# Issue order of two weight groups, one step on VectorE and the count of filler products in the opening of a fused mLSTM and gated MLP kernel

## The chip, the cores and the metric

The kernel runs on one core of a Trainium2 chip. The metric is the time of one execution on the device in microseconds (us). The median of three runs of the kernel before is 516.91 us (516.87 to 516.94).

## The reference

An mLSTM cell (4 batches, 8 heads, 768 steps, head dimension 40) is followed by a gated projection. With x the cell's output as 3072 rows of 320:

```python
for t in range(S):
    m_new = np.maximum(f_gate[:, :, t] + m, i_gate[:, :, t])
    f_stab = np.exp(f_gate[:, :, t] + m - m_new)
    i_stab = np.exp(i_gate[:, :, t] - m_new)
    C = f_stab * C + i_stab * outer(v[t], k[t])
    n = f_stab * n + i_stab * k[t]
    y[t] = sigmoid(o_gate[t]) * (C @ q[t]) / max(abs(n . q[t]), 1)
h = x @ w_in                 # 320 x 2048
out = (h * np.cos(h)) @ w_out  # 2048 x 320
```

All is float32.

## The kernel before, in words

The 768 steps are cut into six chunks of 128. A *cell* n is one chunk of one batch: n = 4 * chunk + batch, 24 cells in all. A cell needs a matrix of decay weights E (loaded as rows of running maxima from DRAM, then exponentials on ScalarE), the scores (`scores`, PE, tile `ps`), their product with E (`weigh`, VectorE), the values (`values`, PE, tile `vt`), the state's increment (`seam`, PE, tile `pu`; `state`, VectorE adds it or ScalarE copies it) and the gated, normalised result xT (`turn_gates`, VectorE).

The projection works on a whole chunk, 512 columns, in eight steps `Up(c, 0)` to `Up(c, 7)`, two tiles `pup` each. For each tile ScalarE rounds (`near`), VectorE takes the rest (`rest`), ScalarE takes the sine (`sin`), and VectorE multiplies (`gate`, tile `g`). `down(c, k)` multiplies g with two 128-row blocks of w_out on PE (16 products of 320 columns, tile `po`, in chunk 0). While a chunk's projection runs, the next chunk's cells are computed between its steps.

The opening loads the weights as well, and works on their bits before they are used: w_in in four groups (`weights_in(0)` to `weights_in(3)`, eight DMAs of 128 KB and two of 128 KB for the low rows each), w_out in eight pieces (`weights_out(0)` to `weights_out(7)`, one DMA of 640 KB each). A piece passes through `take_apart` (two passes on ScalarE, L154 and L156), `bound` (two on VectorE, L160 and L161) and `put_together` (one on VectorE, L167, one on GpSimd, L168); `convert_out()` does all three for the oldest piece of w_out still waiting. Piece p of w_out is used first by `down(0, p)`, group 3 of w_in by `Up(0, 6)`. w_out's pieces rotate through three buffers (the first of them used once for other data before), so piece p waits for piece p - 3; w_in's groups rotate through two.

The program is written under a manual schedule: each engine runs its instructions in the order in which the code issues them, and waits on semaphores where data or a buffer is needed. All loads of this part are issued by SyncE, in order, on one hardware queue.

`warm(k)` issues k products of a tile of zeros (bf16, 128 x 512, L1016, tile `pw`), whose result nobody reads. `gates_turn()` transposes gate tables on PE (L289, L290, tiles `pg`, `pd`), and `gates_keep` copies them on ScalarE. `normalize(3)` is VectorE's work on cell 3 (L621 to L629, tile `y`), `seam(3)` its transposes and increments on PE (L663, L665, L673). `first_cells` is followed by `first_chunk`, in which the projection of chunk 0 runs beside cells 4 to 7.

Of the kernel before, what the change touches and what calls it, by code (L numbers as in the profile page):

```python
# [29 lines left out]
def kernel(  # L30
# [667 lines left out]
    def state(n, part=slice(0, 4), on_dve=False):  # L698
        if n < N - B:
            for j, r, s, w in list(halves(n))[part]:  # L700
                u = increment(n, r, w)
                s = like(s, u)
                if n < B:
                    (nc.vector.tensor_copy if on_dve else nc.scalar.copy)(out=s, in_=u)
                else:
                    nc.vector.tensor_tensor(out=s, in0=s, in1=u, op=OP.add)
# [306 lines left out]
    def warm(k, bank=None):  # L1013

        for _ in range(k):
            nc.tensor.matmul(bank or pw, nil, nil.unsqueeze(1).to_broadcast([128, HP, 128]), start=True, stop=True)  # L1016

    def first_cells():
        gates_in()
        nc.scalar.copy(out=ident_b, in_=ident)  # L1020
        load(0, "qk")
        later_gates_in()
        load(0, "v")
        load(1, "qk")
        load_o(0, (0, 1))
        load(1, "v")
        load(2, "qk")
        load_E(0)
        load_E(1)
        warm(12)  # L1030
        wall_in(0, 0, pmu)
        wall_in(0, 1, psum_o())
        gates_first()
        fill()
        clear_low()
        gates_first_out()
        spread(0, 0)
        decay_exponents_half(0, 0)
        turn(0)
        turn_out(0, False)  # L1040
        gates_sums()
        spread(0, 1)
        decay_exponents_half(0, 1)
        decay(0)
        weigh_k(0)
        load_E(2)
        load(2, "v")
        load_E(3)
        load_o(0, (2, 3))
        load(3)  # L1050
        pieces.extend(weights_in(0))
        wall_in(1, 0, psum_o())
        wall_in(1, 1, psum_o())
        gates_less_sums()
        spread(1, 0)
        decay_exponents_half(1, 0)
        scores(0)
        gates_maxima()
        turn(1)
        weigh(0)  # L1060
        sigmoid(0, slice(0, 2))
        turn_out(1, False)
        spread(1, 1)
        decay_exponents_half(1, 1)
        gates_exponents()
        decay(1)
        weigh_k(1)
        values(0)
        normalize(0)
        scores(1)  # L1070
        turn(2)
        turn_out(2, False)
        gates_exp()
        warm(2)
        seam(0)
        weigh(1)
        seam_out(0)
        state(0)
        load_E(B, and_G=False)
        load_one(B)  # L1080
        decay_exponents(2)
        gates_diagonal()
        decay(2)
        weigh_k(2)
        values(1)
        load_G(B)
        normalize(1)
        scores(2)
        turn(3)
        sigmoid(0, slice(2, 4))  # L1090
        seam(1)
        load(B, "kv")
        outs.append(weights_out(0))
        weigh(2)
        decay_exponents(3)
        turn_out(3)
        seam_out(1)
        values(2)
        decay(3)
        weigh_k(3)  # L1100
        state(1)
        normalize(2)
        warm(2)
        scores(3)
        warm(1)
        seam(2)
        weigh(3)
        take_apart(*pieces[0])
        bound(pieces[0][0])
        put_together(*pieces.pop(0))  # L1110
        values(3)
        decay_exponents(B)
        pieces.extend(weights_in(1))
        seam_out(2)
        state(2)
        for piece in pieces[0:2]:
            take_apart(*piece)
        warm(3)
        pg = gates_turn()
        normalize(3)  # L1120
        gates_keep(*pg)
        bound(pieces[0][0])
        put_together(*pieces.pop(0))
        warm(2)
        seam(3)
        seam_out(3)
        outs.append(weights_out(1))
        load_o(1)
        load_E(B + 1, and_G=False)
        load_one(B + 1)  # L1130
        load(B + 1, "kv")
        load_G(B + 1)
        outs.append(weights_out(2))
        low_dimensions_of(B)
        turn_blocks(B)
        bound(pieces[0][0])
        put_together(*pieces.pop(0))
        state(3, on_dve=True)
        decay(B)
        scale_q(B)  # L1140
        odd_values_of(B)
        weigh_k(B)
        ahead.append(weights_in(2))
# [12 lines left out]
    def convert_out():  # L1156
        piece = outs.pop(0)
        take_apart(*piece)
        convert(*piece)
# [16 lines left out]
    def first_chunk():  # L1176
        n = B
        up = Up(0, 0, lambda: scores(n))
        weigh(n)
        sin_next()  # L1180
        nears(up)
        rests(up)
        sines(up)
        values(n)
        seam(n)
        convert_out()
        outs.append(weights_out(3))
        load_two(n + 2)
        load_E(n + 2)

        up = Up(0, 1)
        full = pieces[0:2]
        low = pieces[2]
        for piece in (*full, low):
            take_apart(*piece)
        for piece in (*full, low):
            bound(piece[0])
        put_together(*full[0])
        nears(up)
        rests(up)  # L1200
        put_together(*full[1])
        sines(up)
        put_together(*low)
        state(n)
        ahead.append(weights_in(3))
        down(0, 0)

        up = Up(0, 2)
        convert_out()
        outs.append(weights_out(4))  # L1210
        load_E(n + 3)
        low_dimensions_of(n + 1)
        turn_blocks(n + 1)
        sigmoid(1)
        nears(up)
        decay_exponents(n + 1)
        rests(up)
        scale_q(n + 1)
        weigh_k(n + 1)
        odd_values_of(n + 1)  # L1220
        sin_next()
        sines(up)
        denominators(n)
        gate_over(n)
        down(0, 1)

        for x in range(2):
            m, f2 = n + x, 3 + 2 * x
            *full, low = ahead.pop(0)
            convert_out()  # L1230
            outs.append(weights_out(5 + 2 * x))
            if x == 1:
                load_two(n + 4, "Kv")
                load_E(n + 4)
            turn_gates(m)
            up = Up(0, f2)
            scores(m + 1)
            take_apart(*full[0])
            decay(m + 1)
            convert(*full[0])  # L1240
            nears(up)
            take_apart(*full[1])
            rests(up)
            convert(*full[1])
            fade(m)
            low_out(m)
            sin_next()
            weigh(m + 1)
            sines(up)
            take_apart(*low)  # L1250
            convert(*low)
            down(0, f2 - 1)
            values(m + 1)
            seam(m + 1)
            if x == 1:
                load_E(n + 5)

            up = Up(0, f2 + 1)
            convert_out()
            if x == 0:  # L1260
                outs.append(weights_out(6))
                load_two(n + 4, "qk")
            else:
                load_o(2)
            state(m + 1)
            if x == 0:
                low_dimensions(n + 2)
                odd_values(n + 2)
            turn_blocks(m + 2)
            decay_exponents(m + 2)  # L1270
            weigh_k(m + 2)
            scale_q(m + 2)
            nears(up)
            rests(up)
            denominators(m + 1)
            sines(up)
            down(0, f2)
            gate_over(m + 1)

        n = 2 * B - 1  # L1280
        convert_out()
        turn_gates(n - 1)
        convert_out()
        up = Up(0, LAST)
        scores(n)
        decay(n)
        fade(n - 1)
        low_out(n - 1)
        decay_exponents(n + 1)
        weigh_k(n + 1)  # L1290
        odd_values(n + 1)
        nears(up)
        rests(up)
        sin_next()
        weigh(n)
        sines(up)
        turn_blocks(n + 1)
        decay(n + 1)
        down(0, LAST - 1)
        values(n)  # L1300
        seam(n)
        load_two(n + 3, "qk")
        load_E(n + 3)
        load_two(n + 3, "Kv")
        for _ in range(6):
            next(last_down)
        denominators(n)
        gate_over(n)
        sigmoid(2)
        sin_next()  # L1310
        turn_gates(n)
        scale_q(n + 1)
        state(n)
        fade(n)
        weight_sums(0)
# [142 lines left out]
```

## Time and profile before

| | |
|---|---|
| median of three runs | 516.91 us (516.87 to 516.94) |
| the profiled execution | 514.89 us |
| its span, first to last instruction | 512.9 us |
| TensorE (PE) busy | 500.8 us (98%) |
| VectorE (DVE) busy | 405.7 us (79%) |
| ScalarE (ACT) busy | 286.3 us (56%) |
| GpSimd (POOL) busy | 247.1 us (48%) |
| mean granted TensorE clock | 0.992 |
| DMA moved | 57.99 MB, of it most in the first 130 us |

The profile is of one execution. A busy engine is one that has an instruction of the program in it; PEld is TensorE's weight load, SPq the issuing of DMAs by SyncE. Idle time of an engine that isn't the bottleneck costs nothing; what matters is who waits last, and the chain of waits follows that back from the end. PEclk is the share of the full clock that TensorE was granted. In lists of waits the columns are the time in total, the number of waits and the longest one.

### The profile page before, as it was taken

What the parts mean: (1) busy time and instruction counts of PE and PEld (TensorE: products, weight loads), DVE (VectorE), ACT (ScalarE), POOL (GpSimd) and SP (SyncE); (2) the same over time, 40 slices, a digit from 0 to 9 for tenths busy, and PEclk for the clock granted to TensorE, in tenths of its full rate; (3) what the DMA queues carried; (4) which work ended last, traced back from release to release, by engine and by line L of the source; (5) the groups of instructions that cost most, each with busy time, mean ns of one, the idle gap of its engine ahead of it and who ended that gap; (6) DMA issues with size and microseconds to landing.
All of it is one profiled execution on the core that took longest, in us unless ns stands there. A gap on an engine that the chain in (4) does not pass through costs nothing.

```text
span 512.9 us, 14114 instructions
## 1 busy us (share of the span) xinstructions
PE 500.8 (98%) x5564; PEld 358.2 (70%) x5564; DVE 405.7 (79%) x831; ACT 286.3 (56%) x550; POOL 247.1 (48%) x413
## 2 busy tenths in 40 slices
PE   9999999899999999999999999999999999999995
PEld 5865554546567787777677777677697677677775
DVE  6898897898598888888878888878878778654644
ACT  3888893957945548635537736538736531323230
POOL 9743645455686585454455354454343333121212
PEclk9989999899999999999999999999999999999999
DMA  9999999998612823922723743733652000001001
GB/s 139 236 204 229 248 188 271 247 207 195 107 55 58 180 79 84 176 58 58 198 45 102 170 74 98 190 56 98 158 86 100 2 6 6 1 1 52 1 2 53
DMA packets 97650, 57.99 MB, mean 113 GB/s; under 512 B 62336, under 2 KB 89056, under 8 KB 97584
## 3 DMA queue, kind: packets, MB, share of 16 engines
q1 hardware_dynamic: 95888, 55.31, 48.8%
q0 software_dynamic: 1360, 1.43, 1.1%
q8 instruction: 44, 0.72, 0.6%
q10 hardware_dynamic: 336, 0.34, 0.2%
q14 instruction: 22, 0.18, 0.1%
HBM read 51.71 MB, written 4.11 MB: 109 GB/s over the span
## 4 chain that ended last, share of the span: by engine, by line
PE 85%; DVE 9%; DMA 2%; issue 1%; ACT 1%; POOL 0%; SPq 0%; DVEq 0%
PE pup L724 32%; PE acc L724 24%; PE pup L783 4%; PE late L724 4%; PE po L822 4%; PE ps L530 4%; PE vt L565 2%; PE vt L556 2%; PE ph L546 2%; PE pw L1016 1%; PE pup L777 1%; PE pu L673 1%; DMA bits<-in_moe_w_in_dram 1%; DVE g L806 1%; DMA bits<-in_moe_w_out_dram 1%
## 5 line engine op out<-in xcount | busy, mean ns | idle before, releaser
L794 ACT ACTIVATE n<-pup 128x512 int32<-128x512 f32 x96 | 52.2, 593 | 179.0 <-PE pup L724 166.5
L724 PE MATMUL pup<-xT,w_in_sb 64*128 64x512 f32 x608 | 147.9, 595 | 0.2 <-DVE g L806 0.2
L797 DVE SCALAR_TENSOR_TENSOR n<-pup,n 128x512 f32<-128x512 f32 x96 | 61.9, 686 | 70.5 <-ACT n L794 70.2
L877 POOL TENSOR_TENSOR D<-g 128x128 f32<-128x128 f32 x40 | 18.9, 473 | 135.1 <-DVE g L806 125.8
L724 PEld LDWEIGHTS pup<-xT,w_in_sb 64*128 64x128 f32 x608 | 59.1, 187 | 35.6 <-issue 32.8
L802 ACT ACTIVATE n<-n 128x512 f32<-128x512 f32 x96 | 58.6, 629 | 14.3 <-DVE n L797 14.3
L806 DVE SCALAR_TENSOR_TENSOR g<-pup,n 128x512 f32<-128x512 f32 x96 | 62.1, 681 | 2.5 <-ACT n L802 1.2
L724 PE MATMUL acc<-w_out_sb,g 64*128 64x160 f32 x624 | 63.6, 296 | 0.0
L724 PE MATMUL acc<-T,g 64*128 64x160 f32 x624 | 61.7, 296 | 0.0
L724 PEld LDWEIGHTS acc<-w_out_sb,g 64*128 64x128 f32 x624 | 55.4, 187 | 8.6 <-issue 8.5
L724 PEld LDWEIGHTS acc<-T,g 64*128 64x128 f32 x624 | 54.0, 187 | 9.7 <-issue 8.9
L453 ACT ACTIVATE E<-E,tab 128x128 f32<-128x128 f32 x160 | 49.0, 388 | 1.3 <-POOL E L439 1.1
L679 POOL DMA_DIRECT2D xL<-xT x38 | 21.3, 562 | 51.6 <-DVE xT L609 40.6
L724 PE MATMUL pup<-xL,w_in_l 64*128 64x512 f32 x152 | 40.2, 589 | 0.0
L724 PE MATMUL acc<-T,S 64*128 64x160 f32 x312 | 39.5, 296 | 0.0
L724 PE MATMUL acc<-w_out_sb,S 64*128 64x160 f32 x312 | 39.2, 296 | 0.0
L822 PE MATMUL po<-w_out_sb,g 128*128 128x320 f32 x128 | 38.4, 454 | 0.4 <-POOL w_out_sb L168 0.4
L783 PE MATMUL pup<-xT,w_in_sb 128*128 128x512 f32 x80 | 37.3, 607 | 0.3 <-DVE xT L609 0.3
L530 PEld LDWEIGHTS ps<-t,t 40*128 40x128 f32 (+1 forms) x384 | 25.5, 187 | 13.8 <-issue 4.9
L822 PEld LDWEIGHTS po<-w_out_sb,g 128*128 128x128 f32 x128 | 24.6, 197 | 13.2 <-issue 1.7
L724 PEld LDWEIGHTS acc<-w_out_sb,S 64*128 64x128 f32 x312 | 30.4, 187 | 3.1 <-issue 3.1
L724 PEld LDWEIGHTS late<-w_out_sb,D 64*128 64x128 f32 x320 | 28.7, 187 | 4.9 <-issue 4.2
(204 smaller groups left out, 959.7 us busy)
## 6 DMA issues: line engine op xcount, KB each, us to landing
E<-M_d SPq DMA_DIRECT2D x22, 512.0 KB, 3.7
qr<-in_q_dram SPq DMA_DIRECT2D x34, 160.0 KB, 3.4
kr<-in_k_dram SPq DMA_DIRECT2D x34, 160.0 KB, 4.4
bits<-in_moe_w_out_dram SPq DMA_DIRECT2D x8, 640.0 KB, 6.6
G<-G_d SPq DMA_DIRECT2D x18, 256.0 KB, 5.5
bits<-in_moe_w_in_dram SPq DMA_DIRECT2D x32, 128.0 KB, 5.0
out_dram<-o_sb SPq DMA_DIRECT2D x22, 160.0 KB, 4.0
o<-in_o_gate_dram SPq DMA_DIRECT2D x40, 80.0 KB, 4.1
```

The costliest lines, as they stand in the source:

```text
L453: nc.scalar.activation(out=Es[n][:, h], in_=Es[n][:, h], func=AF.Exp, scale=-1.0, bias=tab[:, c, 0, g:g + 1])
L530: nc.tensor.matmul(ps[j][:, p], kT[r, p], qT[r, p], start=True, stop=True)
L546: nc.tensor.matmul(ph[:, h], E[:, h], vs(n)[:, h, 0:D1], start=True, stop=True)
L679: nc.gpsimd.dma_start(out=xL[c][64 * e:64 * e + 64, b], in_=ys[n][0:128:2])
L724: ins = nc.tensor.matmul(a, lhs[r], rhs[r], start=start, stop=stop).ins
L783: nc.tensor.matmul(pu.rearrange("p (b t) -> p b t", b=B), w_in_sb[:, i, ts(part_of(f2, e), 128)], xT[c][:, i:NK * B:NK], start=(i == 0 and ...
L794: nc.scalar.activation(out=self.n[e], in_=self.pu[e], func=AF.Copy, bias=0.25)
L797: nc.vector.scalar_tensor_tensor(out=self.n[e].bitcast(FP), in0=self.pu[e], scalar=0.25, in1=self.n[e], op0=OP.add, op1=OP.subtract)
L802: nc.scalar.activation(out=r, in_=r, func=AF.Sin, scale=TWO_PI_DOWN)
L806: nc.vector.scalar_tensor_tensor(out=g, in0=self.pu[e], scalar=TWO_PI, in1=self.n[e].bitcast(FP), op0=OP.mult, op1=OP.mult)
L822: nc.tensor.matmul(po[c][b], gs[c, f][:, ts(b, C)], w_out_sb[:, f], start=(f == 0), stop=(f == NF - 1))
L877: tt(out=D1, in0=G0[:, 1, 1], in1=G1[:, 1, 1], op=OP.add)
```

## The change

Three edits in the opening.

- `first_cells`: `warm(3)` ahead of `gates_turn()` becomes `warm(6)`, and `warm(2)` ahead of `seam(3)` becomes `warm(1)`: three products of zeros more ahead of the gate transposes, one less behind them.
- `first_chunk`: `state(4)` (n is 4 there) moves from ahead of `down(0, 0)` to behind the `convert_out()` of w_out's second piece. On VectorE its four additions come behind the three bit operations of the piece instead of ahead of them.
- `first_chunk`: the ten DMAs of w_in's last group move behind the one of w_out's fifth piece in SyncE's order.

```diff
@@ first_cells
         for piece in pieces[0:2]:
             take_apart(*piece)
-        warm(3)
+        warm(6)
         pg = gates_turn()
         normalize(3)
         gates_keep(*pg)
         bound(pieces[0][0])
         put_together(*pieces.pop(0))
-        warm(2)
+        warm(1)
         seam(3)
         seam_out(3)
@@ first_chunk
         put_together(*full[1])
         sines(up)
         put_together(*low)
-        state(n)
-        ahead.append(weights_in(3))
         down(0, 0)
 
         up = Up(0, 2)
         convert_out()
+        state(n)
         outs.append(weights_out(4))
+        ahead.append(weights_in(3))
         load_E(n + 3)
         low_dimensions_of(n + 1)
         turn_blocks(n + 1)
```

ScalarE's and GpSimd's orders are the same in both programs.

## The prediction

> **What bounds the kernel now.** I read the page first, then PE's waits, then the chain of waits around the longest of them, then stretches of the clock, then the engines' timelines.
>
> ```profile
> span 512.9 us, 14114 instructions
> PE 500.8 (98%) x5564; PEld 358.2 (70%) x5564; DVE 405.7 (79%) x831; ACT 286.3 (56%) x550; POOL 247.1 (48%) x413
> PEclk9989999899999999999999999999999999999999
> ```
>
> TensorE is busy all the time, so an edit is worth what it takes from PE's idle time, or from the time in which PE runs at a lower clock: slices 3 and 8 of 40 show an 8. Who lets PE wait:
>
> ```profile
> PE ps L530 <- DVE xT L609: 2.4, 1, 2.4
> ...
> PE po L822 <- POOL w_out_sb L168: 0.4, 1, 0.4
> ```
>
> One wait of 2.4 us is nearly all that can be had. The chain (start, us, what) shows where it comes from:
>
> ```profile
> 77.10 6.21 DMA bits<-in_moe_w_in_dram
> ...
> 83.37 5.83 DMA bits<-in_moe_w_out_dram
> ...
> 89.23 0.79 ACT w_out_sb L154
> ...
> 92.74 0.57 DVE xT L609
> 93.31 0.04 issue
> 93.36 1.16 PE ps L530 x16
> 94.52 6.19 PE po L822 x16
> ```
>
> w_out's fifth piece is issued at 83.37, behind the ten DMAs of w_in's last group, and lands at 89.20. ScalarE, done with the gates at 84.30, waits 4.9 us for it; VectorE waits for ScalarE, its product xT comes at 93.3, and PE, done with the projection at 90.99, waits for that. Then the clock (stretch, us, PE busy, PEld, DVE, ACT, POOL, clock, DMA share, GB/s):
>
> ```profile
> 30.47:33.87 3.40, 3.40 (x34) 2.86 (x31) 3.18 (x9) 3.34 (x11) 1.24 (x1) 1.00 1.04 196
> 33.88:37.28 3.40, 3.40 (x43) 1.93 (x43) 3.04 (x6) 2.25 (x8) 1.64 (x3) 0.50 0.89 135
> ...
> 91.91:95.30 3.39, 1.95 (x19) 1.65 (x20) 3.08 (x6) 3.38 (x9) 1.63 (x2) 1.00 1.17 210
> 95.32:98.72 3.40, 3.40 (x8) 2.12 (x7) 2.54 (x5) 3.38 (x6) 1.19 (x1) 0.50 1.21 210
> ```
>
> Two stretches of 3.41 us run at half clock; I cut the windows at their edges. They start 61.44 us apart, 18 times their length. The one at 95.3 follows a stretch in which PE had 1.95 us of work. The one at 33.9 follows one without a gap, but filled by small products (16 with 41 columns, ten 32x32 transposes) and only three of 512 columns.
>
> **The change, part by part. 1. The fifth piece ahead of w_in's last group.** The built order shows the one w_out DMA before the ten w_in DMAs, nothing else moved on SyncE.
>
> ```profile
> 76.07 5.49 SPq L177 DMA_DIRECT2D bits<-in_moe_w_in_dram  x8
> ...
> 83.37 0.39 SPq L188 DMA_DIRECT2D bits<-in_moe_w_out_dram  x1
> ```
>
> So its issue moves from 83.37 to about 76.1. Its buffer was the second piece's, which GpSimd left at 60.0: no new wait. Ahead of it remain the rows of E and G, landed by 81.25 (the issue eight behind). Each issue goes on with the landing of the eighth before it: 83.37 comes right after w_in's third DMA landed at 83.31 (77.10 + 6.21). The piece's 640 KB take 2.3 us at the 280 GB/s that this stretch moves (80 to 90 us), 3.4 us at the 194 of the ten us before; it lands at 83.6 to 84.7, about when ScalarE wants it (84.3).
>
> VectorE is free at 86.65 and starts the piece's bit work then, 3.4 us before its 90.05; xT comes at 89.9, ahead of PE's 90.99. **The 2.36 us go.** What is late next: w_in's first half. Its fourth DMA landed by 83.85 (the eighth issue after it); put back by 2.3 to 3.4 us, 86.2 to 87.2. From ScalarE's first pass over it (90.59) to VectorE's last weighing of E (100.11) were 9.5 us, so E would be ready at 95.7 to 96.7, its first half 0.6 us earlier. PE would have done scores (1.1) and the fifth down step (4.5) by 96.6 and wants the first half then. No wait, 0.5 us at the worse end once the other terms have pulled PE forward. I take none, since 280 is the rate of the stretch itself. The second half and the low rows (wanted at 92.5 and about 96) land by 89.2, when the piece landed before, because the sum of bytes is the same. All later transfers keep their place; the sixth to eighth piece landed by 92.6, 95.9 (issues eight behind) and 104.2 and are wanted at 96, 105 and 106 on the shifted clock: over 1 us of slack each.
>
> **2. The clock behind that wait.** Without the gap, the stretch before 95.3 holds 3.4 us of work instead of 1.95. The down step took 6.19 us at half clock; its like at 107.41 took 4.50. **1.69 us go**, if the clock follows PE's work.
>
> The Trainium skill ("TensorE: Matmul & The Clock Gate", the table of its section on why this matters for your kernels) says that half clock comes after idle gaps of over some 3 us. The trace differs: 2.36 us were enough at 91, and no gap at all at 33.9. The same page (Part 1) has a free-running window of 3413 ns, with which the two stretches agree.
>
> **3. Cell 4's state behind the second piece's bit work.**
>
> ```profile
> 55.54 0.85 DVE L706 TENSOR_TENSOR st<-st,pu 40x128 f32<-40x128 f32 x4
> ...
> 57.48 0.83 DVE L167 SCALAR_TENSOR_TENSOR w_out_sb<-bits,w_out_sb 128x640 int32<-128x640 int32 x1
> 58.22 1.13 DVE L511 STREAM_TRANSPOSE t<-qr 128x512 f32<-128x512 f32 x1
> ```
>
> The four additions (0.88 us) change places with the three bit operations (1.8 us). GpSimd's sum, from 58.44 to 60.02, ends 0.88 earlier, at 59.1; PE wants it at 59.7, so its wait of 0.38 us goes. The state itself is read again only at 75 (fade) and its bank only at 69 (the next scores): free. PE does not keep all of it: at 69.26 the scores take the bank that xT left at 68.97, on a VectorE chain that starts from the projection at 59.7 and does not move. **0.28 us stay**; at 74.9 the first half of E is ready 0.6 us before PE wants it, so they pass there.
>
> **4. Zero products.** Three are added ahead of the gate transposes, one is taken from behind them. At 0.225 us each (32.23 to 32.98) six of them end at 33.66; transposes and sums then end at 34.8, the one left at 35.1, the next transposes at 35.45. The last ones wait for VectorE's y at 35.26 either way and start at 35.5, as now: y hides the two added products. If the stretch from 30.46 then counts as work (1.4 us of wide products in place of 0.7), the next is at full clock: the transposes from 35.51 and the sums to 36.93 take 0.36 and 0.48 (as at 29.59) in place of 1.42 together, xT's copy comes 0.26 earlier, and the projection's eight products take 3.54 (as at 47.19), not 3.79. It ends at 40.0 instead of 40.7; scores, low rows and the gate chain follow with slack. **0.7 us go.** If the clock stays low, the two products cost: the transposes end about 0.5 us later. No row shows which number of products decides; I take the gain, because the stretch from 27.05 also had three wide products, with 128-column scores, and kept its clock.
>
> **Sum.** 2.36 + 1.69 + 0.28 + 0.7 = 5.0 us. Behind 100 us PE is the bound (from 150 to 500 it works 349.35 of 350 us), so they stay. The profiled execution took 514.89 (2.0 outside its span); it would take 509.9. The median of the runs stands 2.0 above it; carried over, 511.9. About 0.2% (1 us) can be told from no change.
>
> **Rivals.**
>
> *The clock does not follow.* By the page's rule on gaps the two half-clock stretches have another cause and stay, or they lie elsewhere in other executions (runs and profile do stand 2.0 us apart). Then 2.36 + 0.28 = 2.6 are left, 2.1 with the products' cost: 514.3 to 514.8. For it: a stretch without a gap was followed by half clock. Against it: of all stretches just the one with the long gap and the one with small products. Chance 0.15.
>
> *w_in's first half takes the wait over.* The exponentials queue behind it on ScalarE. Past 86.7 each us is a us of PE's wait ahead of cell 6's values. At 88, 1.3 us: 513.2; at 89 with a half-clock stretch, 2.3 + 1.7: 515.9. For it: DMA share 1.0 and more there. Chance 0.13.
>
> *Slower.* The same place, where the piece holds the queue for its whole time from issue to landing, 6.6 us in the median of the page's eight, so that the first half comes at 90.4. PE waits 3.7 us and pays two half-clock stretches (3.4): 7.1 lost against 5.0 gained, 519.0. It decides from about 90 on. Against it: the queue works on several DMAs at once, and 6.6 is mostly queueing behind others. Chance 0.07.
>
> *The edit does nothing* would need the piece to be held by its buffer: free since 60.0. Chance 0.02.
>
> **How the numbers follow.** The forecast has 0.63: 511.9, from 510.9 (some tenths more in the waits of 0.3 to 0.5 us that PE still has at 127.9 and 135.9 us, and in the lag of 0.25 us behind y) to 512.6. The upper end, 514.8, takes in the first rival and half of the second. Faster by over 0.2%: the forecast, the first rival and most of the second, 0.88. Slower: most of the third, 0.06. Same: 0.06.
>
> **What would show it.** Right: no PE wait for xT near 90; PE's scores of cell 6 about 3.3 us earlier than 93.4, cell 6's values about 5 earlier; the fifth piece landed by 84.7; clock 1.00 throughout; PE's wait for w_out_sb gone. Wrong: ScalarE waiting for w_in near 86 by more than 1 us with a PE wait ahead of the values; a clock of 0.50 near 34 to 38 or 92 to 100; a new PE wait at 100 to 130 us, where the weights of pieces six to eight arrive.

## The result, and the profile after

| | before | after |
|---|---|---|
| median | 516.92 us (516.87 to 517.68, 4 runs) | 511.61 us (510.33 to 512.07, 4 runs) |
| ratio | | 0.989, 95% interval 0.9869 to 0.9911 |
| profiled execution | 514.89 us | 512.07 us |
| its span | 512.9 us | 510.0 us |

The change is 5.3 us faster, against a forecast of 5.0; the median is 0.3 us from the forecast of 511.9. The two profiled executions stand only 2.8 us apart, though: the one of before was 2 us faster than that kernel's median, the one of after 0.5 us slower than its own. That matters below.

The page after, in the lines that were shown of before:

```profile
span 510.0 us, 14118 instructions
PE 498.6 (98%) x5566; PEld 357.1 (70%) x5566; DVE 406.0 (80%) x831; ACT 286.5 (56%) x550; POOL 246.7 (48%) x413
PEclk9999999999999999999999999999999999999998
```

No slice of the opening shows an 8 any more; the one at the very end belongs to the last 3 us. The same two places, each in a window of 3.4 us (columns as before, the clock third from the end), are at full clock now:

```profile
33.88:37.28 3.40, 3.31 (x47) 1.78 (x45) 3.33 (x6) 2.64 (x10) 2.25 (x2) 1.00 0.75 131
...
93.42:96.82 3.40, 3.12 (x12) 1.90 (x10) 3.05 (x6) 3.37 (x7) 0.79 (x2) 1.00 1.07 322
```

PE's waits in the place of the one of 2.4 us:

```profile
PE ps L530 <- DVE xT L609: 0.7, 1, 0.7
PE vt L556 <- ACT spot L1150: 0.7, 1, 0.7
```

So 1.4 us of waiting are left where none was forecast. The second line names a ScalarE step (`spot`), but what PE waits for there is the first half of E: VectorE's first weighing of it ends at 97.11, and the values start at 97.21. The chain between 77 and 91 us says why:

```profile
77.73 9.00 DMA bits<-in_moe_w_out_dram
...
90.26 0.57 DVE xT L609
```

The fifth piece is issued 5.6 us earlier than before, but lands at 86.73, only 2.5 us earlier. ScalarE's waits (total, count, longest) between 40 and 100 us:

```profile
ACT w_out_sb L154 <- DMA bits<-in_moe_w_out_dram: 3.1, 1, 3.1
...
ACT qr L503 <- DMA qr<-in_q_dram: 1.2, 1, 1.2
```

The first line was 4.9 before, the second was not there. And the state behind the bit work:

```profile
55.81 0.83 DVE L167 SCALAR_TENSOR_TENSOR w_out_sb<-bits,w_out_sb 128x640 int32<-128x640 int32 x1
56.55 0.85 DVE L706 TENSOR_TENSOR st<-st,pu 40x128 f32<-40x128 f32 x4
```

They changed places as the edit says, and PE's wait for w_out_sb is gone from its list.

### The profile page after: what moved, and what is told of

Same layout as the page of the kernel before. It is cut to its first block, busy times and chain, and to the rows that moved or that the text cites. A ratio compares the mean times of both kernels' runs of the same rounds, so it can differ in the third digit from the quotient of the medians.

```text
span 510.0 us, 14118 instructions
## 1 busy us (share of the span) xinstructions
PE 498.6 (98%) x5566; PEld 357.1 (70%) x5566; DVE 406.0 (80%) x831; ACT 286.5 (56%) x550; POOL 246.7 (48%) x413
## 4 chain that ended last, share of the span: by engine, by line
PE 78%; DVE 8%; DMA 5%; SPq 3%; ACT 2%; POOL 1%; issue 1%; DVEq 0%; ACTq 0%; POOLq 0%
PE pup L724 32%; PE acc L724 24%; PE late L724 4%; PE ps L530 3%; DMA bits<-in_moe_w_out_dram 3%; PE pup L783 3%; PE vt L565 2%; PE vt L556 2%; PE po L822 2%; SPq L358 1%; DVE g L806 1%; PE pu L673 1%; PE pup L777 1%; DMA ks<-in_k_dram 1%; SPq L333 1%
## 5 line engine op out<-in xcount | busy, mean ns | idle before, releaser
L822 PE MATMUL po<-w_out_sb,g 128*128 128x320 f32 x128 | 36.8, 439 | 0.0
```

Source lines behind the costliest of these rows:

```text
L822: nc.tensor.matmul(po[c][b], gs[c, f][:, ts(b, C)], w_out_sb[:, f], start=(f == 0), stop=(f == NF - 1))
```

## The experiments

Theory 1 is the prediction's: a gap of PE behind the late piece, the half clock that follows the gap, and two small terms that add to them. Theory 2 (the first rival): the half clock has another cause. Theory 3: the pace of the DMA queue decides, through the landing of the fifth piece.

### One part at a time

**The order of the DMAs alone.**

```diff
         state(n)
-        ahead.append(weights_in(3))
         down(0, 0)
 ...
         outs.append(weights_out(4))
+        ahead.append(weights_in(3))
```

> Only w_out's fifth piece ahead of w_in's last group. Theory 1 (the wait for the piece and the half-clock stretch behind it are one loss): 2.4 + 1.7 = 4.1 us less than before, about 512.8; the clock is 1.00 from 92 to 100 and still 0.50 for 3.4 us near 34 to 38. Theory 2 (the clock has another cause and stays): 2.4 less, about 514.5, with 0.50 behind 90. Theory 3 (the pace of the DMA queue decides: ScalarE's wait for the piece only shrinks from 4.9 to 2 or 3 us, as in the profile of the change): 2 to 3 us less in a profile, PE waiting 0.5 to 1 us for xT.

Measured: 511.16 us (509.80 to 513.17, 4 runs) against 517.97 for before beside it (514.27 to 520.12, 19 runs); ratio 0.988, interval 0.9831 to 0.9929. This part alone gives all that the change gives. PE's waits in its profile:

```profile
PE ps L530 <- DVE xT L609: 1.0, 1, 1.0
PE vt L556 <- ACT spot L1150: 0.9, 1, 0.9
```

The clock is at 0.50 from 33.60 to 37.01, much as in the profile of before (33.87 to 37.29), and 1.00 from there to 508 us. The waits are as theory 3 had them, the clock as theory 1. The gain of 6.8 us is above theory 1's 4.1, which still lies in the interval (3.7 to 8.8 us).

**The state alone.**

```diff
-        state(n)
         ahead.append(weights_in(3))
         down(0, 0)
 
         up = Up(0, 2)
         convert_out()
+        state(n)
```

> Only cell 4's state behind the second piece's bit work. PE's wait of 0.4 us for w_out_sb near 60 goes, but with the fifth piece still behind w_in the time is set by its landing near 89: all theories expect 0.0 (within 0.2 us) against before, and PE's wait for xT longer by 0.3. A gain of 0.3 would say that the landing is not what sets the end.

Measured: 517.75 us (515.32 to 521.59, 10 runs), ratio 1.0003, interval 0.9976 to 1.0031: no difference, as expected. But PE's wait for xT grew by 2.8 us, not by 0.3: in this execution the piece landed at 90.76 instead of 89.20, and PE came 1.4 us earlier. So the profile shows what follows a longer wait. First PE's wait, then the windows (clock third from the end):

```profile
PE ps L530 <- DVE xT L609: 5.2, 1, 5.2
```

```profile
92.99:96.39 3.40, 1.50 (x14) 1.50 (x16) 3.30 (x6) 3.37 (x8) 1.56 (x1) 0.50 1.18 168
96.41:99.79 3.38, 3.38 (x12) 2.17 (x11) 2.30 (x6) 3.36 (x8) 1.28 (x1) 0.50 1.10 163
```

The gap of 5.2 us goes with two stretches of half clock. Near 34 us this run has none, although its zeros are those of before.

**The products of zeros alone.**

```diff
-        warm(3)
+        warm(6)
 ...
-        warm(2)
+        warm(1)
```

> Only the products of zeros (6 and 1 in place of 3 and 2). Theory 1: the half-clock stretch near 34 is gone and PE is 0.7 to 1.2 us earlier at 46, but all of it is lost in the longer wait for the fifth piece near 90: 0.0 against before, PE's wait for xT 3 to 3.5 us, perhaps with a further half-clock stretch (1.7 slower). Theory 2: 0.50 near 34 stays, PE's transposes 0.5 later, 0.0 against before as well.

Measured: 517.66 us (515.98 to 518.97, 10 runs), ratio 1.0005, interval 0.9978 to 1.0031: no difference. PE's wait for xT was 4.6 us (expected 3 to 3.5), with one half-clock stretch behind it.

**The change without its zeros** (`warm(3)` and `warm(2)` back).

> The change without its products of zeros (3 and 2 as before). Theory 1: 0.50 near 34 to 38 is back, the rest as the change: 0.7 to 1.2 us slower than the change, if PE and not the DMA queue sets the pace up to 90; about 512.5. Theory 3: the fifth piece's landing sets the pace, so the zeros are worth nothing and this equals the change (511.6) within 0.3.

Measured: 511.74 us (510.44 to 512.94, 4 runs), ratio 0.9888, interval 0.9842 to 0.9934: the change's 511.6 within 0.3, as theory 3 said. The 0.7 us of the zeros don't show at the end, but an interval of 2.4 us to either side could hide them. Its profile had no half clock near 34 either, and ScalarE stood 2.5 us near 55:

```profile
ACT qr L503 <- DMA qr<-in_q_dram: 2.5, 1, 2.5
```

### The piece's place in the queue

All beside one set of 19 runs of before, median 517.58 us (514.08 to 520.35).

**The change again.**

> The change once more, beside the next three. From its first runs: 511.6, between 510.3 and 512.1; about 6 us below the median of before. PE waits 1 to 2 us near 90 to 97 for work that hangs on the fifth piece's landing; no half-clock stretch near 34 or 95.

512.15 us (510.98 to 513.99, 4 runs), ratio 0.9872, interval 0.9830 to 0.9914. The profile has no wait for xT, but 1.3 us ahead of the values and 1.4 us in three waits at the low rows (0.5 of it near 45 us, as in before). Ahead of the values hangs a new wait of ScalarE, for the first half of w_in's last group, at 90.1:

```profile
PE vt L556 <- ACT spot L1150: 1.3, 1, 1.3
...
ACT w_in_sb L154 <- DMA bits<-in_moe_w_in_dram: 0.6, 1, 0.6
```

**Yet earlier**, ahead of the loads for cells 6 and 7.

```diff
         outs.append(weights_out(3))
-        load_two(n + 2)
-        load_E(n + 2)
 ...
         outs.append(weights_out(4))
+        load_two(n + 2)
+        load_E(n + 2)
         ahead.append(weights_in(3))
```

> The change, with w_out's fifth piece yet earlier: also ahead of the loads of cells 6 and 7 (q, k, v, E and G). Theory 1 (what is left of the wait is the piece's landing): ScalarE's wait of 3.1 us for the piece and PE's two waits of 0.7 us near 91 and 97 go: 1.0 to 1.4 us less than the change. Rival (the queue's bytes are the limit, whatever their order): cell 6's k, E or G come 2.5 us later and take the wait over: within 0.3 us of the change, or slower.

511.21 us (510.34 to 511.82, 4 runs), ratio 0.9860, interval 0.9825 to 0.9895. The piece is issued at 64.4, ScalarE takes it at 83.6 without a wait, and PE's two waits are gone. The median is 0.9 us below the change's, but the intervals overlap. ScalarE now waits 1.5 us for w_in, at 86.6, yet PE doesn't wait for what hangs on it. What PE does lose there is 0.9 us at the low rows near 85.8, a wait of 0.3 and 0.6 more within their products. They wait for VectorE, whose small steps L584 and L585 took 1.5 us, against 0.3 in the profile of the earlier piece alone (below); why, the profile doesn't show.

**Amid w_in's last group.**

```diff
-    def weights_in(f):
+    def weights_in(f, amid=None):
 ...
+            if i == 0 and amid:
+                amid()
 ...
-        outs.append(weights_out(4))
-        ahead.append(weights_in(3))
+        ahead.append(weights_in(3, lambda: outs.append(weights_out(4))))
```

> The change, with the fifth piece amid w_in's last group, behind its first four DMAs (512 KB). If each KB ahead of the piece counts, it lands 2 to 2.6 us later than in the change; PE's wait for xT is 2.5 to 3.2 us in place of 0.7, and a half-clock stretch can follow: 2 to 4 us slower than the change, 513.6 to 515.6. Rival (only the low rows and the second half are in the way, or the landing does not set the pace): as the change, within 0.5.

514.10 us (512.42 to 516.92, 10 runs), ratio 0.9938, interval 0.9909 to 0.9967: 2 us slower than the change in the median, still 3.5 faster than before. The chain, the wait and the half clock behind it in its profile, the slowest of its ten runs (two added lines shift the line numbers by 2):

```profile
79.17 10.62 DMA bits<-in_moe_w_out_dram
```

```profile
PE ps L532 <- DVE xT L611: 3.4, 1, 3.4
```

```profile
93.36:96.75 3.39, 2.82 (x18) 2.40 (x19) 2.33 (x5) 3.38 (x11) 1.78 (x2) 0.50 1.12 291
96.78:100.17 3.39, 3.39 (x8) 2.21 (x7) 3.32 (x7) 3.36 (x6) 0.88 (x2) 0.50 1.20 199
```

Four places of one DMA, four times, in order: 511.2, 512.1, 514.1, 517.6 (the last one, before, also has the old state and zeros, which made no difference alone). Each step goes the same way. The last is beyond its interval. The one from the change to the place amid is nearly so (their intervals share 0.9909 to 0.9914), and the first is within the noise.

### The gap and the clock

**Before, with products of zeros in the gap.** Each adds 256 columns of zeros into a tile of sums.

```diff
             up = Up(0, f2)
+            if x == 1:
+                for _ in range(24):
+                    nc.tensor.matmul(po[0][0][:, 0:256].rearrange("p (a n) -> p a n", a=2), nil, nil.unsqueeze(1).to_broadcast([128, 2, 128]), start=False, stop=False)
             scores(m + 1)
```

> Before, with 24 products of zeros (256 columns, 2.6 us) added into a tile of sums ahead of the scores of cell 6, where PE waits for xT; they change no value. Theory 1 (the gap makes the half clock): no stretch of 0.50 behind 95, and since E is ready only 9 us after w_in's first half, not the whole 1.7 us but 0.6 to 1.1 us less than before. Theory 2 (another cause): the stretch stays and the time is that of before within 0.3.

515.80 us (513.27 to 519.02, 10 runs), ratio 0.997, interval 0.9941 to 1.0000: 1.8 us in the medians, not apart from nothing by the interval's end. The profile shows the mechanism. The chain, then a window (clock third from the end):

```profile
90.43 2.62 PE po L1239 x24
93.05 1.09 PE ps L530 x16
94.14 4.50 PE po L822 x16
```

```profile
95.30:98.70 3.40, 3.40 (x17) 2.17 (x19) 3.33 (x7) 3.37 (x7) 0.86 (x2) 1.00 1.21 214
```

The scores begin at 93.05, nearly as late as before (93.36), and yet the down step takes 4.50 us, not 6.19. One profile could be chance, but every execution has its mean clock on record: 0.995 over these ten (0.993 to 0.998) against 0.991 over the 19 of before beside them (0.985 to 0.996). Theory 2 falls: it is the gap that brings most of the half clock.

Over all profiles, waits for xT of 2.4, 3.4, 4.6 and 5.2 us were followed by 3.4, 6.8, 3.4 and 6.8 us of half clock, waits of up to 1.0 us by none. Elsewhere the picture is less clean: a wait of 1.7 us at the low rows was followed by 3.4 us of it (the next section), one of 1.4 us at the same place by none (the change without its zeros), and the place amid has a stretch at 21.7 us behind a wait of only 0.5.

### What the small terms are worth without a late piece

**The earlier piece again, and alone** (cell 4's state and the zeros as before).

> The earlier piece once more, beside the next. From its first runs 511.2, about 0.9 below the change; PE waits for nothing between 60 and 120 us.

> The earlier piece alone: cell 4's state and the products of zeros as before. Now nothing up to 100 us waits for the queue, so what these two edits are worth can show. Theory 1 (the prediction's terms): 0.3 for the state and 0.7 for the zeros, where a half-clock stretch falls near 34: 0.3 to 1.0 us slower than the run beside it. Theory 3 (VectorE, ScalarE and the queue set the pace between 40 and 80, not PE): no difference within 0.3.

Beside each other, before at 516.59 us (514.36 to 519.53, 11 runs): with the two edits 511.85 us (510.33 to 513.17, 6 runs), ratio 0.9902, interval 0.9871 to 0.9933; without them 510.67 us (509.65 to 512.73, 6 runs), ratio 0.9889, interval 0.9855 to 0.9923. The median is 1.2 us lower without them, where theory 1 expected it 0.3 to 1.0 higher; six runs each are too few to tell 0.3 from nothing. And the profile without them has no half clock near 34, so there the zeros had nothing to take away. Nor did PE wait for nothing in the first of them: its profile has a wait of 1.7 us at the low rows near 64 and a half-clock stretch right behind it, at 66.9; ScalarE had stood 2.5 us for q's rows at 55:

```profile
PE pup L777 <- DVE g L806: 2.2, 2, 1.7
...
ACT qr L503 <- DMA qr<-in_q_dram: 2.5, 1, 2.5
```

The lowest median of all is that of the earlier piece alone, but no interval separates it from the change.

## Why the prediction was right, and where it was not

**Right: what bounds the kernel, and the first two terms.** The piece's landing was the one wait worth having, and the half clock behind it belongs to it. The order alone gives the whole gain, a filled gap takes the half clock away, and a piece put amid w_in's group gives 3.5 of 5.4 us. The first rival (the clock does not follow) and the slower one (the piece holds the queue) did not come.

The rule of the Trainium skill on gaps above some 3 us ("TensorE: Matmul & The Clock Gate", section "Why this matters for your kernels") did not hold here: 2.4 us were enough. The free-running window of 3413 ns that the Trainium skill describes on the same page (Part 1) fits better still after the experiments. Divided by 3.413, the starts of the stretches, counted from the span's start (33.87, 33.60, 92.98, 95.77 in four profiles), leave 3.15, 2.88, 0.83 and 0.20: another phase in each, while the two stretches of one profile (33.87 and 95.31) share theirs.

**Wrong in size: where the piece lands.** The forecast was 83.6 to 84.7; it was 86.73. The transfer itself was sized well: the seventh w_in DMA, which goes on with the landing of G's last rows, is issued at 83.92, and the piece lands 2.8 us after that (forecast 2.3 to 3.4). The step that failed took the landing of G, 81.25, from the profile of before; in the profile after it is 83.9. The queue was later there from early on: the first issue at this place is at 77.73, not 76.07, and the third piece's at 56.45, not 55.10. Hence the 1.4 us of waits in place of none, and 2.8 us between the two profiles in place of 5.0. PE's scores of cell 6 came 2.5 us earlier (forecast 3.3), cell 6's values 3.4 us earlier (about 5).

**The second rival came in part.** It had w_in's first half take the wait over, ahead of cell 6's values. The forecast landed that half at 86.2 to 87.2; ScalarE started on it at 88.16 in the change's first profile, right behind the piece, and at 90.14 in the second, after a wait of 0.6 us. From there to VectorE's last weighing of E were 9.5 us in both, as the prediction had it, so PE's waits ahead of the values, 0.7 and 1.3 us, hang on that start. This is the same error carried on: w_in stands behind the piece, and with G's landing late both are.

**Not shown: the terms of 0.28 and 0.7 us.** No run shows either at the end: not alone, not beside the new order, and not taken away from the version with the earlier piece, though intervals of over 1 us to either side could hide terms of this size. Further up the traces do show gains, and PE gives them back at the next landing: in the profile after it starts the last projection step ahead of cell 6's scores 0.9 us earlier than before (86.44 against 87.30), and then it waits.

From cell 4's scores to cell 5's, near 40 and 69 us, PE takes 28.5 us in the five profiles with the state in its old place. It takes 28.3 in the two with the state behind the bit work in which ScalarE never waits for q's rows (yet earlier, amid): that is the term. In the five others with the state behind, ScalarE stands 0.6 to 2.5 us for q's rows near 55 and PE takes 28.5 to 32.1 us, through ScalarE's steps on the projection and the low rows that wait for them. The prediction did not look at q's rows. In the profile of before, the first of them landed at 53.96 and ScalarE took them at 55.21, so there was no wait to see; in the profile after, they landed at 55.20, and ScalarE, 1.2 us earlier by then, stood for them.

The half clock near 34 is real: from cell 3's scores to the w_in products of the second projection step PE takes 19.4 us with it (before, order alone) and 18.3 to 18.8 in the ten profiles without. But it came in two of the six profiles with the old zeros and in none of the six with the new ones; too few to say that the zeros prevent it.

**Why the total fits all the same.** Two errors cancel, and that is luck. The small terms, 1.0 us, don't show at the end; but the first two are worth more than the 4.1 us counted in the profile of before, which was one of that kernel's quick executions (514.89, where 49 other executions in three sets had medians of 516.6 to 518.0). In two other profiles with the old order the wait was 4.6 and 5.2 us with one and two stretches of half clock.

The clocks on record give an estimate of the split. The share of the clock that wasn't granted, times the span, is 4.7 us in the mean of those 49 executions and 1.5 us in the eight of the change (this takes PE to be at work wherever the clock was low). So about 3 us of the 5.3 are clock, where the prediction counted 1.69 for the stretch behind the wait and 0.7 for the other one. Carrying the 2.0 us between profile and median over as a constant was a choice that the prediction did not justify: going by these profiles and clocks they are mostly the usual wait and its half clock, which no run shows by itself.

**Open.** Why the queue's pace differs by 2 to 3 us at 80 us from execution to execution. It differs long before the edit on the queue: SyncE's order up to w_out's third piece is the same in all twelve programs, and that piece is issued at 54.2 to 57.8 us, at 55.61 and 57.77 in two profiles of one program. The queue is at its fullest there: the first 130 us move 28 of the 58 MB, just under half and not most of them, at 216 GB/s against 78 behind. No run here changed the pace, and so the differences between the versions with the early piece (medians of 510.7 to 512.2) could not be settled.

## What to carry to other kernels

Where a transfer's landing ends a wait, move its issue and count the bytes that stay ahead of it; but take its landing from several executions, because one profile can be at the quick end of a spread that is as large as the gain. A gap on TensorE can cost itself and then the half clock behind it, so look at the clock behind each gap. Small gains ahead of a stretch that waits for a queue end at that queue: ask of each term which transfer it meets next, before adding it to the sum.

## What the runs showed of the hardware

- A gap of 2.4 us on TensorE was followed by 3.4 us at half clock, one of 4.6 us by as much, and ones of 3.4 and 5.2 us by 6.8 us; one of 1.7 us was followed by 3.4 us, one of 1.4 us by none. 24 products of zeros in the gap (2.6 us) left the clock at 1.00 in the profile, and the mean clock over the runs was 0.995 in place of 0.991.
- In two profiles a stretch in which TensorE was busy for all of its 3.4 us, much of it with small products, was followed by half clock; the same products in four other profiles were not.
- Issuing a 640 KB transfer 5.6 us earlier, where the DMA engines' share was 1.0, brought it in only 2.5 us earlier: from issue to landing it took 5.8 us at its old place, 9.0 us ahead of w_in's group and 10.6 us amid it, in one profile each.
- The executions of one program spread over 6 us (before, 514.1 to 520.4 in 19 runs) and over 4 us (the change, 510.3 to 514.0 in eight). The late transfer alone does not set the spread: the zeros alone, with the same late transfer, spread over 3 us in ten runs.
